# Conformer block on one core: threads for the last two chunks, and output products that yield to background work

## The chip, the cores and the metric

One of the eight cores of one Trainium2 chip runs the kernel. The metric is the device time of one execution in microseconds (us). Engines: PE is TensorE (matmul), PEld its weight loads, DVE VectorE, ACT ScalarE, POOL GpSimd, SP SyncE. The granted clock is the clock at which PE ran by the trace's records, as a share of its full speed; half-clock time is time at 0.5.

## The reference, cut to what matters

```python
B, T, D, K, H = (2, 4000, 144, 5, 4)
h = silu(layernorm(x) @ w_ff1a) @ w_ff1b;   x = x + 0.5 * h          # first feed-forward
q, k, v = split(layernorm(x) @ w_qkv)                                # 4 heads of 36
p = softmax(q @ k^T * scale)                                         # 4000 x 4000 per head and batch
x = x + (p @ v) @ w_o
a, b = split(layernorm(x) @ w_pw1);  h = a * sigmoid(b)              # GLU
x = x + silu(depthwise_conv5(h)) @ w_pw2
h = silu(layernorm(x) @ w_ff2a) @ w_ff2b;   x = x + 0.5 * h          # second feed-forward
return layernorm(x)
```

The softmax needs 2 x 4 x 4000 x 4000 exponentials. The other activations are few beside them.

## The kernel before

The 8000 tokens are 16 chunks of 500. For each chunk there are 63 key tiles; each of the 1008 pairs costs four score matmuls into two PSUM banks ("S"), one exponential over 128 x 1000 elements into a PT tile ("E"), and four output products ("O") that add PT times V to the chunk's two output banks. Most exponentials run on ACT as one ACTIVATE; some are computed on DVE by integer and polynomial steps.

The program is written by a planner. While the kernel is built, it simulates the engines with fixed costs per instruction and decides at each step which instruction comes next; the order is then fixed, and each engine has its own list. The other layers are "background": threads (Python generators) that ask for an engine and a buffer, one step at a time.

```python
def post2(c):                       # second half of a chunk's life
    z = yield need("pe", swp, cond=lambda: c in glu_done and (last or c + 1 in glu_done))
    ...                             # convolution of chunk c into SW buffer z (needs the GLU of c + 1)
    ...                             # pointwise product, residual, layer norm, transposes
    yield from ff(c, s, WA2, WE2, WB2, "W2", mode["tail"], store)     # second feed-forward, final norm

def series(gens):                   # one thread that works through several chunks
    for g in gens:
        yield from g
...
for par in range(2):                # two series: even chunks, odd chunks
    S.add(series(post2(c) for c in range(par, NCH, 2)), R.last, rank=2)
```

So chunk 15 can begin its second half only when chunk 13 has finished its own. The choice for PE, where `o` are output products that are ready, `s` the next scores, `ok` background steps that fit ahead of the time at which ACT would run dry, and `ptp` the 7 PT tiles:

```python
if R.kind == "q" and o and (not s or ts + 0.3 < deadline):
    return o[0]                                    # attention running: output products first
if ok:
    return min(ok, key=lambda q: not q[2].req.hold)
if s:
    return s[0]
```

The middle's layer norms use POOL; the planner's costs (in us) are the `cost` arguments:

```python
yield need("pool")
op("pool", "tensor_scalar", ..., op0=ALU.add, ..., cost=0.25)          # variance + eps
op("pool", "tensor_tensor", ..., op=ALU.pow, ..., cost=0.7)            # to the power -0.5
if not (mode["front"] or mode["tail"]):
    op("pool", "tensor_scalar", ..., op0=ALU.mult, ..., cost=0.3)      # -mean
    for j in range(n):                                                 # four blocks
        op("pool", "tensor_scalar", XN[...], ..., op0=ALU.add, op1=ALU.mult, ..., cost=0.55)
```

After the last output product comes the tail, with no exponentials left (`mode["tail"]`: silu on ACT directly, layer norms on DVE). In the names of the profile, PS is PSUM, QT and KT queries and keys, VA values, OTF a copy of the output banks, XN a normalised block, XT its transpose, WA/WE/HT/WB the feed-forward (first-layer weights, hidden, second-layer weights), U and DG the convolution, SW its result, WP and WP2Z the pointwise product, TH a tanh.

The softmax here doesn't subtract the row's maximum and nothing guards it: scores larger than these inputs give would overflow.

## Time and profile before

| | before |
|---|---|
| time, median of 4 runs | 1030.56 us (1030.09 to 1031.57) |
| span of the profiled execution | 1026.3 us |
| end of the last exponential on ACT | 967.0 us |
| tail, from there to the end of the span | 59.3 us |
| ACT idle from 100 to 955 us (855 less its busy time) | 12.7 us |
| half-clock time of PE: before the last exponential ended, in the tail | 0, 42.7 us |

The page of the kernel before, its parts 1, 2, 4 and 5: busy us, share of the span and instructions by engine; the granted PE clock in 40 slices, in tenths; the chain of work that ended last, by engine; and two groups of instructions (busy us and mean ns of one, then idle time before them):

```profile
PE 924.8 (90%) x11294; PEld 365.0 (36%) x11294; DVE 788.0 (77%) x2092; ACT 945.8 (92%) x1175; POOL 283.3 (28%) x562
...
PEclk9999999999999999999999999999999999999956
...
ACT 65%; PE 22%; DVE 9%; POOL 2%; issue 1%; DMA 1%; ACTq 0%; POOLq 0%; DVEq 0%
...
L158 ACT ACTIVATE PT<-PS 128x1000 bf16<-128x1000 f32 x914 | 851.9, 1041 | 11.5 <-PE PS L158 9.8
...
L158 DVE TENSOR_SCALAR ZB<-PS 128x500 uint16<-128x500 f32 x188 | 118.5, 672 | 33.2 <-PE PS L158 31.9
```

ACT carries two thirds of the chain, and 914 exponentials are nine tenths of its work. There are two ZB instructions for each exponential on DVE, so 94 of them. Every line number is L158 because a helper issues all instructions; tile names tell them apart. The PE clock is full until the last two slices.

The stretches of the kernel before (us from the start; busy us and instructions of each engine in the stretch; then granted PE clock, DMA share, GB/s):

```profile
100.00:955.00 855.00, 789.68 (x9945) 295.51 (x9944) 678.19 (x1672) 842.32 (x1023) 236.47 (x454) 1.00 0.01 4
...
967.00:984.00 17.00, 11.25 (x81) 7.43 (x79) 11.54 (x40) 4.84 (x9) 4.42 (x14) 0.69 0.00 1
984.00:992.00 8.00, 7.69 (x49) 5.26 (x47) 1.12 (x6) 3.20 (x7) 0.01 (x1) 0.60 0.00 0
992.00:1004.00 12.00, 8.38 (x41) 5.06 (x42) 5.68 (x26) 3.90 (x7) 3.79 (x8) 0.58 0.05 13
1004.00:1020.00 16.00, 10.10 (x60) 6.22 (x58) 6.67 (x30) 4.64 (x9) 3.83 (x8) 0.71 0.03 10
```

The columns after the stretch's length are PE, PEld, DVE, ACT, POOL. From 100 to 955 ACT works 842.3 of 855 us. In the tail no engine but PE (in the 8 us from 984) comes near full, and PE's clock is 0.6 to 0.7. The timeline of PE in that tail (start, length in us, instruction; in brackets the idle time before it and what ended it) shows why it is long:

```profile
982.53 2.70 PE L158 MATMUL PS<-XT,WA 72*128 72x500 bf16 x6
...
996.42 3.52 PE L158 MATMUL PS<-XT,WA 72*128 72x500 bf16 x8 [0.68 <-ACT XT L158]
...
1001.24 2.66 PE L158 MATMUL PS<-WB,HT 128*125 128x144 bf16 x20 [0.47 <-ACT HT L158]
1003.69 1.62 PE L158 MATMUL PS<-U,DG 128*128 128x500 bf16 x12
...
1012.31 3.52 PE L158 MATMUL PS<-XT,WA 72*128 72x500 bf16 x8 [0.68 <-ACT XT L158]
```

Three feed-forwards follow one another (chunks 13, 14, 15, first layer at 982.5, 996.4 and 1012.3), and the convolution of chunk 15 (U,DG at 1003.69) waits for its series, though its GLU was done at 984.

Who waited for whom from 100 to 955 (waits of PE, then of ACT; us in total, times, longest):

```profile
PE PS L158 <- POOL XN L158: 2.0, 3, 1.0
...
ACT PT L158 <- PE PS L158: 8.6, 27, 1.0
```

### The profile page before, as it was taken

Reading aid. Unit: us, or ns where it says so; the run is one execution under the profiler, and the core shown is the slowest. Engines: PE = TensorE matmul, PEld = TensorE weight load, DVE = VectorE, ACT = ScalarE, POOL = GpSimd, SP = SyncE. Lnnn points to the kernel's source line nnn. Section 1 sums busy time; section 2 is a strip of 40 time slices with the busy share of each in tenths; the row PEclk is TensorE's granted clock in tenths of the full one; section 3 lists DMA queues with packets and bytes.
Section 4 is the critical chain, followed back from the end, with each engine's and each line's share of the span. In section 5 each row is a group of like instructions: output and inputs, shape, how many; then the busy total and the mean of one; then the engine's idle time right before and its main releaser. Section 6 shows DMA issues by size and latency. Waiting matters only on the chain.

```text
span 1026.3 us, 26612 instructions
## 1 busy us (share of the span) xinstructions
PE 924.8 (90%) x11294; PEld 365.0 (36%) x11294; DVE 788.0 (77%) x2092; ACT 945.8 (92%) x1175; POOL 283.3 (28%) x562
## 2 busy tenths in 40 slices
PE   7899989998999999998999999999999988998775
PEld 4444333333334333433333332333333333343343
DVE  6976877888966987787888778968886987666843
ACT  3899999999999999999999999999999999999741
POOL 3321313114324333320422132321513212223222
PEclk9999999999999999999999999999999999999956
DMA  4000000000000000000000000000000000000000
GB/s 130 3 1 2 2 2 2 1 2 2 1 2 2 2 2 2 7 2 2 2 7 2 7 7 2 2 8 7 8 2 8 2 7 7 2 8 7 7 6 12
DMA packets 7419, 7.31 MB, mean 7 GB/s; under 512 B 2349, under 2 KB 7300, under 8 KB 7300
## 3 DMA queue, kind: packets, MB, share of 16 engines
q1 hardware_dynamic: 6144, 5.14, 1.7%
q8 instruction: 88, 1.44, 0.6%
q10 hardware_dynamic: 1156, 0.47, 0.2%
q14 instruction: 31, 0.25, 0.1%
HBM read 3.31 MB, written 2.30 MB: 5 GB/s over the span
## 4 chain that ended last, share of the span: by engine, by line
ACT 65%; PE 22%; DVE 9%; POOL 2%; issue 1%; DMA 1%; ACTq 0%; POOLq 0%; DVEq 0%
ACT PT L158 59%; PE PS L158 22%; ACT TH L158 5%; DVE ZB L158 2%; DVE ST L158 1%; DVE MB L158 1%; DVE HT L158 1%; POOL RS L158 1%; DVE X L158 1%; POOL XN L158 1%; DMA WQKV<-in_w_qkv_dram 1%; DVE XT L158 1%; DVE PT L158 0%; DVE XN L158 0%; DVE MV L158 0%
## 5 line engine op out<-in xcount | busy, mean ns | idle before, releaser
L158 ACT ACTIVATE PT<-PS 128x1000 bf16<-128x1000 f32 x914 | 851.9, 1041 | 11.5 <-PE PS L158 9.8
L158 PE MATMUL PS<-QT,KT 64*64 64x500 bf16 x4032 | 397.4, 391 | 50.3 <-ACT PT L158 29.5
L158 PE MATMUL PS<-PT,VA 64*37 64x500 bf16 x4032 | 366.1, 373 | 10.5 <-ACT PT L158 7.0
L158 POOL TENSOR_SCALAR RS<-MV 125x4 f32<-125x4 f32 (+1 forms) x160 | 46.3, 289 | 668.3 <-DVE MV L158 662.7
L158 PEld LDWEIGHTS PS<-QT,KT 64*64 64x64 bf16 x4032 | 116.8, 103 | 306.5 <-ACT PT L158 219.9
L158 DVE TENSOR_SCALAR ZB<-PS 128x500 uint16<-128x500 f32 x188 | 118.5, 672 | 33.2 <-PE PS L158 31.9
L158 PEld LDWEIGHTS PS<-PT,VA 64*37 64x37 bf16 x4032 | 105.7, 95 | 71.9 <-ACT PT L158 42.7
L158 POOL TENSOR_SCALAR XN<-X,RS 125x144 bf16<-125x144 bf16 x228 | 127.6, 572 | 5.9
L158 ACT ACTIVATE TH<-PS 128x500 bf16<-128x500 f32 (+2 forms) x195 | 103.6, 538 | 8.0 <-PE PS L158 7.7
L158 DVE SCALAR_TENSOR_TENSOR HT<-TH,PS 128x500 bf16<-128x500 bf16 (+1 forms) x135 | 82.3, 618 | 32.4 <-ACT TH L158 31.5
L158 DVE SCALAR_TENSOR_TENSOR X<-PS,X 125x288 bf16<-125x288 f32 x128 | 56.9, 452 | 58.0 <-PE PS L158 57.3
L158 POOL TENSOR_TENSOR RS<-RS,NHALF 125x4 f32<-125x4 f32 (+1 forms) x103 | 97.6, 948 | 8.6
L158 PE MATMUL PS<-XT,WA 72*128 72x500 bf16 x256 | 77.7, 402 | 5.7 <-DVE HT L158 2.3
L158 DVE TENSOR_SCALAR MB<-MB 128x1000 f16<-128x1000 f16 x188 | 78.0, 415 | 1.5
L158 DVE BATCH_NORM_STATS2 ST<-X 125x6 f32<-125x144 bf16 x320 | 75.2, 294 | 0.4
L158 DVE TENSOR_TENSOR PT<-ZB,MB 128x1000 bf16<-128x1000 bf16 x94 | 66.0, 702 | 2.2
L158 DVE TENSOR_TENSOR MB<-MB 128x1000 f16<-128x1000 f16 x94 | 63.8, 679 | 2.1
L158 PE MATMUL PS<-WB,HT 128*125 128x144 bf16 x640 | 63.1, 241 | 2.5 <-ACT HT L158 1.5
L158 PEld LDWEIGHTS PS<-WB,HT 128*125 128x125 bf16 x640 | 49.4, 143 | 37.4 <-issue 22.6
L158 PE MATMUL PS<-IDENT,XN 125*72 125x125 bf16 x512 | 44.1, 226 | 15.0 <-DVE XN L158 11.7
L158 DVE COPY XT<-PS 72x1000 bf16<-72x1000 bf16 (+1 forms) x65 | 40.1, 617 | 11.7 <-PE PS L158 10.6
L158 PEld LDWEIGHTS PS<-IDENT,XN 125*72 125x72 bf16 x512 | 32.4, 115 | 40.8 <-DVE XN L158 15.2
(78 smaller groups left out, 682.0 us busy)
## 6 DMA issues: line engine op xcount, KB each, us to landing
X<-in_x_dram SPq DMA_DIRECT2D x16, 140.6 KB
out_dram<-XN SPq DMA_DIRECT2D x13, 140.6 KB
out_dram<-XN SPq DMA_DIRECT2D x6, 70.3 KB
WA<-in_w_ff1a_dram ACTq DMA_DIRECT2D x1, 144.0 KB
WB<-in_w_ff1b_dram ACTq DMA_DIRECT2D x1, 144.0 KB
WA<-in_w_ff2a_dram SPq DMA_DIRECT2D x1, 144.0 KB
WB<-in_w_ff2b_dram SPq DMA_DIRECT2D x1, 144.0 KB
WQKV<-in_w_qkv_dram ACTq DMA_DIRECT2D x1, 121.5 KB
```

What stands on the lines that cost most here:

```text
L158: ins = getattr(eng, o.name)(*o.a, **o.k)
```

## The change

Its intent: shorten the tail by letting the last two chunks end side by side, and let background work get on earlier while there is no pressure on PT tiles, so that less of it is left over.

```diff
-    NXN, NXT, NTH, NHT, NSW = 5, 5, 4, 3, 2
+    NXN, NXT, NTH, NHT, NSW = 5, 5, 4, 3, 3
...
+    ALONE = 2
+    OFREE = 4
...
-        if R.kind == "q" and o and (not s or ts + 0.3 < deadline):
+        if R.kind == "q" and o and (not s or ts + 0.3 < deadline) and not (ok and len(ptp.free) >= OFREE):
             return o[0]
...
             for par in range(2):
-                S.add(series(post2(c) for c in range(par, NCH, 2)), R.last, rank=2)
+                S.add(series(post2(c) for c in range(par, NCH - ALONE, 2)), R.last, rank=2)
+            for c in range(NCH - ALONE, NCH):
+                S.add(post2(c), R.last, rank=2)
```

Below, "the threads" are the last hunk and "the rule" is the condition with `OFREE`.

## The prediction

> **What bounds the kernel now.** By the page, ACT is busy 945.8 us (92%), PE 924.8 (90%), DVE 788.0 (77%). By windows, from 420 to 967 us ACT is busy 543.0 of 547: ACT's stream alone bounds the middle (idle 4 us; about 14 from 40 to 420). The timeline shows 21 exponentials in 19.11 us, 0.91 each; the Trainium skill, "ScalarE: Activation LUTs" (What ACT_TABLE_LOAD costs: 186 ns + 0.833 ns per element, less 93 overlapped), gives 0.93 for 1000 elements, which agrees. The last exponential ends at 967. From there to 1026.3 is a tail of 59 us in which no engine is full and the granted PE clock falls to 0.5 to 0.7.
>
> **The tail before.** 967 to 984 is chunk 15's epilogue up to its GLU. Then second feed-forwards run one after another: chunk 13 (983 to 991), 14 (996.4 to 1003.9), 15 (1012.3 to 1019.8), the last two each behind an exposed layer norm. Chunk 15's convolution starts only at 1003.7: it is in one series behind chunk 13.
>
> **What the change does.** (a) Chunks 14 and 15 are threads of their own; with a third SW buffer they start together. (b) Ready output products yield to background PE work while 4 or more of 7 PT tiles are free. No arithmetic is added. The instruction order of the built kernels shows:
> - exponentials on ACT 914 to 908, on DVE 94 to 100 (some 5 us of DVE each, off the critical path);
> - after the last exponential: HT activations 15 to 10, 500-column first-layer matmuls 24 to 16; of chunk 13's feed-forward only its last tiles and 20 output matmuls remain;
> - both convolutions and pointwise products together, then feed-forward 14, then 15, whose transposes come before 14's output: no layer norm exposed between;
> - before the last exponential three more 500-column tanh on ACT, three fewer copies;
> - isolated output products 708 to 451, groups of 2 to 5 instead; 30 more switches between attention and background.
>
> **Cost on the critical path.** Middle: 6 exponentials x 0.91 = -5.5; three tanh x 0.48 (start to start) and a small one, +1.7; copies -1.5: about -5 us. Idle ACT time (18 us) may change either way; I count 0.
> Tail: second-layer matmuls now end at 1019.8. After, from the same 984: convolutions 2 x 1.6, SW and pointwise products to 991, layer norm to 996.5 (as before), two feed-forwards of 7.5 (4.4 first layer, 0.5 wait, 2.7 output, at the measured low clock): 1011.5, so -8.3 us. Chunk 13's rest after the last exponential may give back 1 us.
> Sum: about -13 us.
>
> **Prediction: 1017.5 us**, 8 in 10 between 1009 and 1026. Chances: faster by over 2% 0.14, within 2% 0.83, slower by over 2% 0.03.
>
> **What would show it.** 908 exponentials on ACT; the last ending near 962; ACT idle from 100 to 960 within 4 us of before. From the last exponential to the end about 51 us instead of 59; feed-forward 15 directly behind 14, PE idle between under 1 us; chunk 15's convolution right after its GLU. If the last exponential stands at 967 or later, the output rule starved ACT: its waits for scores (8.6 us from 100 to 967 now) or for free PT tiles would have grown.
>
> **What would make it wrong.** If real durations differ from those the order was built for, longer output runs hold up scores; more DVE exponentials could delay layer norms and evictions; the front's schedule changes too and may shift by several us; a still lower tail clock would lengthen both feed-forwards.

## The result, and the profile after

| | before | after | predicted |
|---|---|---|---|
| time, median of 4 runs | 1030.56 us | 1017.42 us (1015.6 to 1019.75) | 1017.5 us (1009 to 1026) |
| end of the last exponential | 967.0 | 969.5 | 962 |
| tail | 59.3 | 46.7 | 51 |
| ACT busy until the last exponential | 929.2 | 920.9 | about 924 |
| ACT idle, 100 to 955 | 12.7 | 22.8 | within 4 us of before |
| half-clock time before the last exponential ended, in the tail | 0, 42.7 | 20.5, 34.6 | not predicted; "low clock" in the tail |

The ratio of the times is 0.9872 (95% interval 0.985 to 0.9895). Ratios here are the mean time of one kernel's fast runs over that of the other's of the same rounds, so not quite the ratio of the quoted medians. The change is faster by 1.3%, clear of the noise. The sum was right almost to the microsecond, but two of its terms were not: the middle gained nothing, and the tail gained more than foreseen. The errors cancelled.

The page after, in the same parts:

```profile
PE 913.4 (90%) x11294; PEld 393.1 (39%) x11294; DVE 811.1 (80%) x2144; ACT 934.5 (92%) x1165; POOL 298.5 (29%) x565
...
PEclk8999899999999999999999999999999999999967
...
ACT 51%; PE 28%; DVE 13%; POOL 5%; issue 1%; DMA 1%; ACTq 0%; POOLq 0%; DVEq 0%
...
L158 ACT ACTIVATE PT<-PS 128x1000 bf16<-128x1000 f32 x908 | 843.2, 1045 | 21.7 <-PE PS L158 20.2
...
L158 DVE TENSOR_SCALAR ZB<-PS 128x500 uint16<-128x500 f32 x200 | 126.1, 672 | 45.4 <-PE PS L158 43.9
```

Six exponentials moved from ACT to DVE, as the built order had shown. But ACT now sat idle 20.2 us before exponentials for want of scores (9.8 before), ACT's share of the chain fell from 65 to 51%, and the PE clock has dips at the first and fifth slices, where before it had none.

Stretches after:

```profile
100.00:955.00 855.00, 778.61 (x9913) 319.85 (x9913) 697.36 (x1725) 832.24 (x1013) 252.51 (x461) 0.99 0.01 4
117.90:121.40 3.50, 1.79 (x24) 0.36 (x16) 3.36 (x16) 3.50 (x5) 3.33 (x6) 1.00 0.02 5
121.40:131.60 10.20, 9.26 (x66) 3.35 (x70) 6.29 (x10) 6.04 (x8) 4.26 (x8) 0.50 0.00 0
...
998.00:1005.00 7.00, 7.00 (x38) 4.68 (x39) 1.01 (x4) 3.31 (x6) 0.71 (x1) 0.50 0.00 0
1005.00:1010.00 5.00, 4.12 (x37) 2.74 (x35) 3.77 (x15) 2.30 (x5) 1.91 (x4) 0.96 0.06 18
```

The second and third lines are the largest single loss in the middle. PE was busy only 1.79 of 3.5 us, then its clock was halved for 10.2 us, in which ACT worked 6.0. What PE waited for just before, in its timeline after:

```profile
121.53 1.05 PE L158 MATMUL PS<-IDENT,XN 125*72 125x125 bf16 x8 [0.77 <-POOL XN L158]
123.36 1.01 PE L158 MATMUL PS<-XT,WA 72*128 72x500 bf16 x2 [0.78 <-DVE XT L158]
...
127.97 2.30 PE L158 MATMUL PS<-PT,VA 64*37 64x500 bf16 x20
```

A transpose of a normalised block stood in PE's list ahead of output products that were ready; POOL was late with the block, PE ran nothing from 120.8 us until it came, and five tiles' output products (x20) later came in one lump. But the wait for POOL is only a part of PE's idle time here (0.6 us of 1.7 before the clock fell), and e3 will show that this loss has another cause in the main. The clearest case of late POOL is at 718 us, where PE waited 2.28 us for a block and ACT then 1.95 us for scores:

```profile
720.42 0.63 PE L158 MATMUL PS<-IDENT,XN 125*72 125x125 bf16 x8 [2.28 <-POOL XN L158]
...
721.43 1.90 ACT L158 ACTIVATE PT<-PS 128x1000 bf16<-128x1000 f32 x2 [1.95 <-PE PS L158]
```

The waits from 100 to 955 after, of PE and of ACT:

```profile
PE PS L158 <- POOL XN L158: 6.2, 6, 2.3
...
ACT PT L158 <- PE PS L158: 18.8, 36, 2.2
```

The tail after, PE's timeline:

```profile
986.89 4.98 PE L158 MATMUL PS<-U,DG 128*128 128x500 bf16 x24 [1.54 <-POOL U L158]
...
997.93 3.51 PE L158 MATMUL PS<-XT,WA 72*128 72x500 bf16 x8 [0.68 <-ACT XT L158]
...
1002.91 2.61 PE L158 MATMUL PS<-WB,HT 128*125 128x144 bf16 x20
1005.31 1.92 PE L158 MATMUL PS<-XT,WA 72*128 72x500 bf16 x8
1007.07 0.59 PE L158 MATMUL PS<-XT,WE 72*128 72x250 bf16 x4
1008.34 1.46 PE L158 MATMUL PS<-WB,HT 128*125 128x144 bf16 x20 [0.68 <-ACT HT L158]
```

Both convolutions now stand together (x24) and feed-forward 15 follows 14 without a gap, as predicted. Not predicted was the time of the last one: its first layer took 1.92 us where the same eight matmuls took 3.51 us just before, because the clock came back at 1005.4.

### The profile page after: what moved, and what is told of

It reads as the page before. It is cut to its first block, busy times and chain, and to the rows that moved or that the text cites. A ratio compares the mean times of both kernels' runs of the same rounds, so it can differ in the third digit from the quotient of the medians.

```text
span 1016.2 us, 26673 instructions
## 1 busy us (share of the span) xinstructions
PE 913.4 (90%) x11294; PEld 393.1 (39%) x11294; DVE 811.1 (80%) x2144; ACT 934.5 (92%) x1165; POOL 298.5 (29%) x565
## 4 chain that ended last, share of the span: by engine, by line
ACT 51%; PE 28%; DVE 13%; POOL 5%; issue 1%; DMA 1%; ACTq 0%; POOLq 0%; DVEq 0%
ACT PT L158 45%; PE PS L158 28%; ACT TH L158 5%; DVE ZB L158 3%; POOL XN L158 3%; POOL RS L158 2%; DVE MB L158 2%; DVE ST L158 2%; DVE HT L158 1%; DVE X L158 1%; DVE XT L158 1%; DMA WQKV<-in_w_qkv_dram 1%; DVE MV L158 1%; DVE PT L158 0%; DVE XN L158 0%
## 5 line engine op out<-in xcount | busy, mean ns | idle before, releaser
L158 ACT ACTIVATE PT<-PS 128x1000 bf16<-128x1000 f32 x908 | 843.2, 1045 | 21.7 <-PE PS L158 20.2
L158 PE MATMUL PS<-QT,KT 64*64 64x500 bf16 x4032 | 391.2, 387 | 39.1 <-ACT PT L158 27.0
L158 PE MATMUL PS<-PT,VA 64*37 64x500 bf16 x4032 | 338.9, 378 | 21.5 <-ACT PT L158 16.5
L158 POOL TENSOR_SCALAR RS<-MV 125x4 f32<-125x4 f32 (+1 forms) x160 | 49.8, 311 | 623.1 <-DVE MV L158 617.2
L158 PEld LDWEIGHTS PS<-QT,KT 64*64 64x64 bf16 x4032 | 119.2, 104 | 236.5 <-ACT PT L158 156.5
L158 DVE TENSOR_SCALAR ZB<-PS 128x500 uint16<-128x500 f32 x200 | 126.1, 672 | 45.4 <-PE PS L158 43.9
L158 POOL TENSOR_SCALAR XN<-X,RS 125x144 bf16<-125x144 bf16 x232 | 135.1, 594 | 6.1
L158 DVE TENSOR_SCALAR MB<-MB 128x1000 f16<-128x1000 f16 x200 | 83.2, 416 | 1.6
L158 DVE TENSOR_TENSOR PT<-ZB,MB 128x1000 bf16<-128x1000 bf16 x100 | 69.2, 692 | 2.0
L158 DVE TENSOR_TENSOR MB<-MB 128x1000 f16<-128x1000 f16 x100 | 68.4, 684 | 2.2
```

The lines of the kernel that those rows point to most:

```text
L158: ins = getattr(eng, o.name)(*o.a, **o.k)
```

## The experiments

The table gathers the measurements; the runs follow one by one. "Idle" is ACT's from 100 to 955 us (855 less the busy time in that stretch), from the one profiled execution of each kernel; half-clock time is from the clock records of the same trace, counted to the end of the span. (Some expectations quote 36.7 us for the tail after; that count ran 2 us past the span's end.) Each kernel's ratio is to the kernel before in the same rounds; that kernel's median was 1029.33 to 1030.15 us in the later rounds and 1030.56 in the first, so compare kernels of different rounds by their ratios. After, e2 and e4 have one order up to the tail, and so have before, e1 and e8: the spread within these (last exponential 969.5 to 971.0 and 966.5 to 969.7, idle 22.8 to 24.0 and 12.4 to 13.0) is what one profile can be off at least. All results were correct.

| run | time, us (4 runs) | ratio | exponentials on ACT | last one ends | tail | idle | half clock in the tail |
|---|---|---|---|---|---|---|---|
| before | 1030.56 | | 914 | 967.0 | 59.3 | 12.7 | 42.7 |
| after | 1017.42 | 0.9872 | 908 | 969.5 | 46.7 | 22.8 | 34.6 |
| e1 threads only | 1021.93 | 0.9937 | 914 | 966.5 | 52.1 | 12.4 | 31.6 |
| e2 rule only | 1017.69 | 0.9895 | 908 | 971.0 | 46.5 | 23.9 | 35.3 |
| e3 after, POOL cost | 1015.76 | 0.9872 | 905 | 964.3 | 50.8 | 17.0 | 33.8 |
| e4 after, tail filled | 1013.46 | 0.9842 | 908 | 971.0 | 40.6 | 24.0 | 4.6 |
| e5 both | 1010.01 | 0.9809 | 905 | 962.7 | 44.5 | 16.0 | 3.7 |
| e6 threads, POOL cost | 1026.63 | 0.9968 | 915 | 972.9 | 52.0 | 13.4 | 26.2 |
| e7 after, other order | 1019.52 | 0.9905 | 905 | 972.6 | 45.3 | 25.9 | 24.8 |
| e8 threads, tail filled | 1013.52 | 0.9841 | 914 | 969.7 | 43.4 | 13.0 | 1.4 |
| e9 fitted | 998.03 | 0.9698 | 902 | 957.3 | 38.9 | 15.7 | 1.2 |
| e10 fitted, more fill | 998.06 | 0.9693 | 902 | 957.6 | 38.8 | 16.0 | 0.2 |
| e11 fitted, no rule | 1014.11 | 0.9852 | 916 | 972.6 | 39.1 | 13.2 | 1.0 |

### e1 and e2: the parts of the change alone

Two controls needed no chip. Built with the third SW buffer alone, the kernel has the same instruction order as before on every engine; and the threads give the same order with two SW buffers as with three. The third buffer does nothing by itself. (Both, and the whole change with two buffers, were built again when this text was checked: apart from the addresses of the SW buffers, all instructions are the same.)

e1 keeps the threads and drops the rule:

```diff
-        if R.kind == "q" and o and (not s or ts + 0.3 < deadline) and not (ok and len(ptp.free) >= OFREE):
+        if R.kind == "q" and o and (not s or ts + 0.3 < deadline):
```

> Threads for chunks 14 and 15 and the third SW buffer, without the output-product rule. The instruction order differs from the kernel before only after the last exponential. Theory A (the rule moves chunk 13's feed-forward out of the tail, the threads only remove the series): the last exponential ends at 967 as before, 914 exponentials, chunk 13's feed-forward still stands whole in the tail, so the tail is 52 to 55 us and the time 1023 to 1026. Rival B (the prediction's reading: the two threads make the tail gain): tail about 51 us, time 1022 or less.

Measured: 1021.93 us, last exponential at 966.5, tail 52.1 us. The middle stayed as it was, and the threads took 7.3 us off the tail, close to the predicted 8.3 (rival B's numbers, at the edge of A's).

e2 keeps the rule and drops the threads:

```diff
-    NXN, NXT, NTH, NHT, NSW = 5, 5, 4, 3, 3
+    NXN, NXT, NTH, NHT, NSW = 5, 5, 4, 3, 2
...
-    ALONE = 2
+    ALONE = 0
```

> The output-product rule alone; chunks 14 and 15 in the old series, two SW buffers. The order up to the last exponential is the changed kernel's, instruction for instruction. Theory A: chunk 13 is out of the way by then, so the series costs nothing: within 2 us of the changed kernel, 1015 to 1020. Rival B (threads needed): the tail goes back to about 55 us or more, time 1023 or more.

Measured: 1017.69 us, tail 46.5 us. That is the changed kernel's time, within the noise (the intervals of the ratios overlap). With the rule, chunk 13 is nearly done when the tail begins and the old series holds up nobody. So the two parts do not add: either shortens the tail, the rule by 12.8 us, the threads by 7.3, and given the rule the threads bring nothing that these runs can see. Rival B was right about the threads alone and wrong about the whole change.

### e3, e6, e7: why the middle gained nothing

The question was why ACT's idle time rose by 10 us. Theory C: background matmuls that the rule puts ahead of ready output products wait, in order, for POOL. The planner allows 0.7 us for the power step, while its mean for four blocks in the trace is 1131 ns before and 1161 after (for two blocks, as in the tail, 722 and 723); the planner sees the transposes ready too early. Before the change this mattered little (waits of 2.0 us), because the ready output products went first and covered the delay. The power step in the trace of the kernel before:

```profile
L158 POOL TENSOR_TENSOR RS<-RS,NHALF 125x4 f32<-125x4 f32 x57 | 64.4, 1131 | 4.7
L158 POOL TENSOR_TENSOR RS<-RS,NHALF 125x2 f32<-125x2 f32 x46 | 33.2, 722 | 3.8
```

Rival D: longer runs of output products hold up scores. Rival E: any reshuffle of a tuned order costs this much.

e3 is the changed kernel with an edit of the planner's cost alone. (The 1.5 us is a margin above the measured 1.13 to 1.16, so e3 tests later placement, not the exact cost.)

```diff
-           r=[("VE", u), "NHALF"], w=[("RS", u)], cost=0.7)
+           r=[("VE", u), "NHALF"], w=[("RS", u)], cost=1.5)
```

> The changed kernel, with the planner's cost of the POOL power step raised from 0.7 to 1.5 us (about what the trace shows of the whole POOL chain), so that transposes that need POOL's result are placed later. Theory C (ACT's extra idle time in the middle comes from background matmuls that now stand ahead of ready output products and wait in order for late POOL results, down to halving PE's clock): ACT idle from 100 to 960 falls from 22.7 us to 17 or less, PE's waits for POOL XN there from 6.2 to under 3 us, time 1010 to 1014. Rival D (longer runs of output products hold up the scores) or E (any reshuffle of the order costs this much): idle stays at 20 us or more, time 1015 to 1020.

Measured: idle 17.0 us; PE's waits for POOL XN are no longer among its waits from 100 to 955; the last exponential ended at 964.3, 5.2 us earlier. The line of the same stretch in e3:

```profile
100.00:955.00 855.00, 781.25 (x10010) 319.96 (x10002) 713.91 (x1768) 838.02 (x1021) 244.01 (x464) 1.00 0.01 4
```

The order has as many runs of three and more output products as the changed kernel (90 against 91), which speaks against D as the main cause. The time, 1015.76, missed the 1010 to 1014 that was expected: the tail was 4 us longer than after, and in it the clock stayed at half for the whole of the last 23.6 us, so the last feed-forward did not get the full clock that it had got after. By their ratios (0.9872 both) the two kernels are level.

e6 is the same cost with the threads but without the rule:

> Control for the POOL cost: threads only, without the output-product rule, with the POOL cost of 1.5 us. Theory C (the idle time and its cure belong to the rule): little to cure, ACT idle from 100 to 960 stays near 12 us (within 3), no half-clock time before 960, time 1019 to 1025. Theory E (any reshuffle of the order costs or saves this much): idle moves by 5 us or more from 12.4.

Measured: idle 13.4 us against 12.4 in e1. The cost cures nothing where the rule does not run, as C says. The rest of the expectation failed: 17.1 us of half clock before the last exponential (13.7 of it before 100 us, where ACT was idle 28.9 us against 25.1), and the time was 1026.63, worse than e1 by 4.7 us in the medians and by some 3 us in the ratios. In this one order the front lost 3.8 us of it; that is kept in mind for e9.

e7 is the changed kernel with another tie-break, which changes the order in thousands of places but no policy:

```diff
-    PW = 0.12
+    PW = 0.125
```

> Control for reshuffling: the changed kernel with the planner's choice window at 0.125 instead of 0.12 us, which changes the order in thousands of places but no policy and no POOL cost. Theory C: the rule and the optimistic POOL cost are still there, so ACT idle from 100 to 960 stays above 19 us and PE's waits for POOL XN above 4 us. Theory E: idle anywhere between 12 and 25, unrelated to the waits for POOL.

Measured: idle 25.9 us and waits of PE for POOL XN of 8.1 us. That line of e7's waits, from 100 to 960 us:

```profile
PE PS L158 <- POOL XN L158: 8.1, 8, 2.3
```

A different order with the same rule and the same optimistic cost loses the same way. Over the runs (two different orders of each kind with the rule, three without), idle time goes with the pair rule plus optimistic cost (22.8, 23.9, 24.0, 25.9) against rule plus raised cost (17.0, 16.0, 15.7, 16.0) against no rule (12.4 to 13.4). Theory C accounts for some 6 to 7 of the 10 us. Of the 3 to 4 us that the rule costs even with the raised cost, most lie in one place, the stretch shown above as the largest single loss. Here it is before, after and in e3:

```profile
115.00:140.00 25.00, 22.69 (x260) 7.14 (x261) 20.19 (x57) 24.94 (x31) 6.87 (x14) 1.00 0.01 2
115.00:140.00 25.00, 21.53 (x214) 8.00 (x213) 19.79 (x56) 20.54 (x26) 8.22 (x14) 0.80 0.00 1
115.00:140.00 25.00, 20.41 (x218) 7.28 (x210) 21.10 (x62) 21.57 (x27) 8.83 (x14) 0.86 0.01 1
```

ACT is idle 0.1, 4.5 and 3.4 us of these 25 (2.5 in e9), although e3 has no wait for POOL XN left. PE's clock falls to half in this stretch in every run with the rule and in none without it but e6 (3.4 us); so this loss goes with the rule, not with POOL's cost. Which part of the rule causes it was not tested; D may be part of it.

### e4, e5, e8: the clock in the tail

e4 fills PE's gaps in the tail of the changed kernel with matmuls into a PSUM bank that nobody reads (the tail's own work loses that bank; `FILL` is 0.3 us):

```diff
-    for i in (BX, BX + 1):
-        banks.free[i] = R.last
+    banks.free[BX] = R.last
...
-        S.run(next(th for t, th in c if t <= lim))
+        t, th = next((t, th) for t, th in c if t <= lim)
+        if th.req.eng == "pe" and o_count[NCH - 1] == NT and len(outs) < NCH + 3:
+            while R.free["pe"] + FILL < t:
+                op("pe", "matmul", PSV[:, BX + 1, 0:CH], lhsT=IDENT[:, :], rhs=KT[:, 0, 0, 0:CH], start=True,
+                   stop=True, skip_group_check=True, r=["ID", ("WKT", 0)], w=[("ps", BX + 1)], cost=c_pe(CH), kind="f")
+        S.run(th)
```

> The changed kernel, with matmuls into an unused bank put into PE's gaps after the last output product; results unchanged. Theory F (the tail's length is set largely by PE's halved clock): half-clock time in the tail falls from 36.7 us to under 10, the tail from 46.9 to about 40 us, time about 1010. Rival G (the tail is a chain of layer norms and evictions, PE's clock is a side effect): under 2 us gained, or some lost, 1016 to 1021.

Measured: 1013.46 us; half-clock time in the tail 4.6 us instead of 34.6, tail 40.6 us. The time missed the expected 1010: the middle, the same order as after, ended 1.5 us later in this profile. PE's timeline of e4, to compare with the one after:

```profile
987.68 2.66 PE L158 MATMUL PS<-U,DG 128*128 128x500 bf16 x24 [1.33 <-POOL U L158]
...
996.45 1.87 PE L158 MATMUL PS<-XT,WA 72*128 72x500 bf16 x8
...
999.43 1.46 PE L158 MATMUL PS<-WB,HT 128*125 128x144 bf16 x20
1000.73 1.86 PE L158 MATMUL PS<-XT,WA 72*128 72x500 bf16 x8
```

The clock of e4 in such a stretch (1.00, where from 998 to 1005 us after it was 0.50):

```profile
996.00:1001.00 5.00, 4.93 (x45) 3.13 (x44) 1.73 (x8) 3.13 (x7) 0.93 (x2) 1.00 0.00 0
```

The convolutions take 2.66 us instead of 4.98, the first layer of feed-forward 14 takes 1.87 instead of 3.51. Theory F holds: the clock, not only the chain of norms, sets the tail's length. The Trainium skill, "TensorE: Matmul & The Clock Gate" (Part 1), says that the activity gate passes either the full or half the clock and changes after windows of about 3.4 us; the clock records of these traces agree: only 1.0 and 0.5 occur, for 3.41, 6.83 or 10.24 us and other multiples of 3.41 (the last, cut off by the end of the span, apart).

e5 joins e3 and e4:

> The two edits of the last runs together: the POOL cost of 1.5 us and the filling matmuls in the tail. If they act on different stretches, the middle's end stays near 964 (as with the POOL cost alone) and the tail near 41 us (as with the fill alone): about 1005 span, time 1006 to 1009, faster than before by over 2%. If the earlier last exponential of the POOL-cost kernel was luck of one profile, or is given back in the tail, time stays at 1012 or more.

Measured: 1010.01 us. The last exponential was at 962.7, so e3's gain in the middle came again (in the same order); the tail was 44.5 us, 3.9 longer than in e4, and the time missed its range. Two things differ. The clock fell to half for 3.4 us just as the convolutions began, which took 4.32 us against 2.66 in e4. And in the tail a power step handles two blocks and takes 719 ns by e5's trace, so a cost of 1.5 makes the planner fill too much: seven filling matmuls stood between the two halves of a chunk's transposes where e4 had three. PE's timeline of e5, with the convolutions, the seven and the second half of the transposes:

```profile
979.26 4.32 PE L158 MATMUL PS<-U,DG 128*128 128x500 bf16 x24 [1.53 <-POOL U L158]
...
988.37 1.64 PE L158 MATMUL PS<-KT,IDENT 128*128 128x500 bf16 x7
989.84 0.39 PE L158 MATMUL PS<-IDENT,XN 125*72 125x125 bf16 x4
```

e8 puts the fill of e4 into e1 (threads, no rule):

> Threads only, with the filling matmuls in the tail: the middle as before (last exponential near 967). If the rule's use is only to take chunk 13 out of the tail, and PE's clock made that dear, then with a warm clock chunk 13's feed-forward costs little and the tail is 43 to 45 us: time 1011 to 1014, level with the rule plus fill (1013.5). If the rule is worth more than that, 1016 or more.

Measured: 1013.52 us and a tail of 43.4 us, as expected. With the clock kept up, the extra feed-forward of chunk 13 costs 2.8 us (43.4 against 40.6 in e4), where at the low clock it cost 5.4 (52.1 against 46.7). The two kernels are level, but not because the rule is worth nothing: the rule takes some 8 us of work off ACT (920.9 against 929.2 up to the last exponential, after and before) and gives it back as idle time (13.0 against 24.0). The last exponential came at 969.7, not near 967 as expected: this execution had 10.2 us of half clock in its first 26 us.

### e9, e10, e11: a version that beats both, and what the rule is worth there

e9 is e5 with the cost confined to the middle, where the power step handles four blocks:

```diff
-           r=[("VE", u), "NHALF"], w=[("RS", u)], cost=1.5)
+           r=[("VE", u), "NHALF"], w=[("RS", u)], cost=0.7 if mode["front"] or mode["tail"] else 1.5)
```

> The rule, threads, tail fill, and the POOL cost of 1.5 us only between front and tail (in the tail a power step takes 0.72 us in the traces, so 1.5 there put 7 filling matmuls where 2 or 3 fit and held up the transposes). If that is why the tail of the last combination was 44.5 us and not 41: tail 41 us or less, last exponential 961 to 966, time 1004 to 1008. If not: tail stays at 44 us, time 1008 to 1011.

Measured: 998.03 us (996.71 to 999.92), ratio 0.9698, better than expected in both parts: tail 38.9 us, last exponential at 957.3. The tail fits the reading of e5: three filling matmuls stand between the halves again. But the lapse of the clock at the convolutions is gone too, so the run does not part the two. For the middle, the built order has 902 exponentials on ACT and 106 on DVE, and ACT's busy time up to the last exponential is 915.8 us, 13.4 less than before and 6.0 less than in e5: three exponentials and four copies fewer on ACT, at the same idle time. No expectation had foreseen that order; this part of the gain was found by trying. The same stretch in e9:

```profile
100.00:955.00 855.00, 782.77 (x10050) 321.42 (x10053) 730.39 (x1802) 839.33 (x1022) 248.38 (x468) 1.00 0.01 4
```

DVE is busy 730.4 of 855 us (678.2 before), PE 782.8: DVE has taken over work that ACT had.

e10 adds six filling matmuls ahead of the tail's first convolution:

```diff
             bk = yield need("pe", banks, dur=0.22)
+            if not filled:
+                filled.append(c)
+                for _ in range(6):
+                    op("pe", "matmul", ...)            # as in e4, but cost=0.05
```

> As the run before it, with six filling matmuls ahead of the first convolution of the tail, where PE waits some 1.5 us for halo copies and its clock fell to half for 3.4 us. If that lapse costs time, the tail is 1 to 2 us shorter than in the run before it; if the convolutions are not on the chain, no difference within 1 us.

Measured: 998.06 us, tail 38.8 us, no difference. There was nothing to save: in e9 the lapse that e5 had at that point did not occur (its only half-clock time in the tail is the last 1.2 us).

e11 takes the rule out of e9 (the number of stores after which filling ends was adapted):

> The fitted combination without the output-product rule: threads, tail fill, POOL cost of 1.5 us between front and tail. The built order has 916 exponentials on ACT (902 with the rule), and chunk 13's feed-forward is out of the tail here too. If the rule is worth what its exponentials are (14 x 0.91 us and a few tanh more): last exponential at 968 to 972, tail 39 to 40 us, time 1008 to 1013, 10 us or more above the fitted combination. If the POOL cost and the fill made the gain and the rule is worth nothing: within 3 us of 998.

Measured: 1014.11 us, last exponential at 972.6, tail 39.1. The time is 1 us above the range, the last exponential 0.6, and the time is 16 us above e9, all of it in the middle: 916 exponentials on ACT against 902, at 13.2 us idle against 15.7. So the rule is worth a good deal, once the planner's costs let ACT keep what it gains.

## Why the prediction was right or wrong, point by point

- **What bounds the kernel**: right. ACT's stream sets the middle, and the tail is a chain of its own. The prediction's estimate from the Trainium skill, "ScalarE: Activation LUTs" (What ACT_TABLE_LOAD costs), 0.93 us for 1000 elements back to back, was borne out within 3%: 15 exponentials in 13.51 us after, 0.90 each.
- **Fewer exponentials and what moves**: right in count, 908, since the built order shows it. ACT's work until the last exponential fell by 8.3 us rather than 5.3; the page shows 8.7 us less for exponentials though only six were gone. That extra was not looked into.
- **"Idle ACT time (18 us) may change either way; I count 0"**: wrong, and the step that failed. It rose by 10 us and ate the whole gain of the middle: the last exponential ended at 969.5 instead of 962. The prediction named the sign to look for (waits for scores above 8.6 us; they became 18.8). It also named, as what would make it wrong, durations that differ from the planner's. But the mechanism it had in mind, long runs of output products that hold up scores, was not the main one: for 6 to 7 of the 10 us the rule removed the slack that had covered the planner's optimistic POOL cost (e3 against e6 and e7). Most of the rest is one stall at 115 to 140 us, which PE's halved clock stretched (ACT idle 4.5 us after, 3.4 in e3) and whose cause stays open.
- **The tail's size, -8.3 us**: mis-sized; it was -12.7. The term is "two feed-forwards of 7.5": feed-forward 14 took 7.4 us (997.9 to 1005.3), feed-forward 15 only 4.5 (to 1009.8), as the clock had come back; the convolutions and the norm (986.9 to 997.9) took 11.0 us against 12.5 counted, and the way there 17.4 against 17. e4 shows what the clock does there.
- **What makes the tail gain**: half right. The prediction derived the tail from the built order of the whole change, and that order came about; but it told the story of the threads, while e2 shows that the rule alone gives it all, and e1 that the threads alone give 7.3 us.
- **The time**: right at 1017.42 against 1017.5, with errors of +7.5 us in the middle and -4.3 us in the tail. In the two profiles the span fell by 10.1 us, 3.2 less than the predicted 13.3; in the medians the time fell by 13.1, because the profiled execution of the kernel before (1028.12 us) was 2.4 us faster than that kernel's median and that of the kernel after (1017.98) 0.6 slower. So the agreement to 0.1 us is partly luck. One more observation: four runs of the changed kernel spread over 4.2 us (before: 1.5), and the fastest, 1015.6 us, had the highest mean clock (0.978), the two slowest the lowest (0.973). Clock lapses that come and go from run to run are part of this kernel's spread.

## What to carry to other kernels

If one instruction list is fixed ahead of time, a rule that puts waiting work before ready work is only as good as the cost it assumes for the producer: look for waits on the one engine whose cost was guessed low, and raise that cost before judging the rule (here 16 us with the raised cost and the filled tail, e9 against e11; nothing with the old cost, e4 against e8). In a tail where PE is half idle, look at the granted clock, and try matmuls into an unused bank to keep it up. And when a predicted total comes out right, check its terms: here two errors of several us cancelled, and finding them was worth more than the change itself (998.0 against 1017.4 us).

## What the Trainium skill lacked or had wrong

- "TensorE: Matmul & The Clock Gate": the table of practical rules tells of a drop to half clock after PE idle gaps of about 3 us (the section on a second failure mode tells of micro-idles, without a figure). Here the clock fell at 121.4 us after a stretch in which no single gap was longer than 0.8 us: PE was busy 1.79 of the 3.5 us before (51%). Partial idleness within one window was enough.
- The same page: it gives no figure of how busy PE must be within a window to keep the full clock. The profile's busy share of one window does not settle it either: the clock fell after 2.48 busy us of 3.41 (after, from 967.87 us) and stayed full after 1.92 of 3.41 (before, from 1004.12 us). Filling matmuls in the gaps were enough here (half-clock time in the tail 34.6 to 4.6 us).
- "GPSIMD Engine Reference" has no duration for a power step on few elements: 125x4 f32 took 1131 ns on average, 125x2 took 722 ns. Planning it at 0.7 us cost most of what the rule gained in the middle (idle 22.8 to 25.9 us; 15.7 to 17.0 with a higher cost).
